# An adaLN transformer block on one core: the order of its first loads, of one gate row and of the last output tile

## The chip, the cores and the metric

The kernel runs on one core of a Trainium2 chip. The metric is the device time of one execution in microseconds (us). A core has five engines with queues of their own: PE (TensorE, matrix products into PSUM), DVE (VectorE), ACT (ScalarE), POOL (GpSimd) and SP (SyncE, which here only issues DMAs). ACT also issues some DMAs. All DMAs run on the same 16 DMA engines, in one queue for those that SP issues and another for those that ACT issues.

## The reference

One sequence of S = 2048 rows with D = 448 columns, bf16. The cut reference:

```python
mod = (silu(c) @ w_mod).reshape(1, 6, 1, -1)          # sa, ca, ga, sb, cb, gb: shifts, scales, gates
h = layernorm(x) * (1 + ca) + sa
# A: linear attention, 16 heads of 28; phi(p) = [softmax(p w_phi), softmax(-p w_phi)]
kv, z = phi_k^T v, sum(phi_k)                          # key-value sums, per head
o = (phi_q kv) / (phi_q z);  x = x + ga * (o @ wo)
h = layernorm(x) * (1 + cb) + sb
# B: gated MLP, F = 1792, halves of 896
z1, z2 = split(gelu(h @ w_in));  z2 = layernorm(z2)
g = w_sp @ z2 + b_sp                                   # mixes the 2048 rows
out = x + gb * ((z1 * g) @ w_out)
```

## The kernel before

The rows are cut into 16 tiles of 128. The body, `fast_path`, is a set of small functions ("steps"), each of which issues a few instructions, and a string, `ORDER`, in which every word is one call: `name:arguments@slot/engine`. The instructions of an engine run in the order of the words; nothing reorders them. A slot is a place in PSUM: A0, A1, A2 hold two banks each, B0 and B1 one; a step that writes a slot waits until the last reader of what was there is done. The engine letters are V (DVE), S (ACT), G (POOL), Y (SP). `ld:x/Y` is a load issued by SP, `ld:x/S` one issued by ACT. A DMA's issue also waits until the DMA eight places before it has landed, since there are eight semaphores for them.

The stages and the steps that matter here:

- **Start** (up to some 12 us). `du:n` are n warm-up matmuls of 256 columns on the zeroed tile `zero`; they compute nothing that is used. `ct` turns the row c by PE, `ce:1` to `ce:4` make silu(c) of it, `csA` and `ccA` are 16 one-column products each that give shift and scale as columns. `FTk`, `ETk`, `FSk`, `FCk`, `PFk`, `EPk` fold w_phi, shift and scale into the key weights `f_Wk`. `l1s`, `l1e`, `l1r`, `l1a` are the first layernorm (DVE statistics, POOL power, then the scaled tile into `f_xpad`), `X:i` turns tile i by PE into `f_hT`.
- **Key-value sums** (some 12 to 53 us). For every tile `kM` (keys), `kE`, `kF` (two exponentials on ACT), `kS` (sums on DVE), `kR`, `kP` (normalised keys, on DVE or POOL), `vM`, `vC` (values), `kA` (adds to the sums in PSUM). In between stand `qM:n`, the query products for half of the heads over 512 rows, with `qF:n` and `qE:n`, their exponentials on ACT. `gr:0` and `gr:1` are the two gate rows (four products of 448 columns each, from `f_wmg`), `ge` their copies to SBUF; `wos:k` multiplies gate row 0 into part k of wo, `wts:k` gate row 1 into part k of w_out. `T1` are DMA transposes of layernormed tiles.
- **Joint.** When `kA:15` is done, `KV` and `KZ` take the sums out of PSUM, and the attention starts.
- **Attention and z** (some 55 to 138 us). `nM:i` (numerators), `nX`, `nC`, `nS`, `nT`, `nA` (their weights, on ACT, DVE, POOL), `T2` (DMA transposes of the result), `wM:i` (times wo), `wR`, `wQ`, then the second layernorm (`l2R`, `l2r`, `l2a`, `T3`) and the products with w_in: `zM`, `yM`. `csB`, `ccB` are shift and scale for it. `W:t,u` are DMA transposes of blocks of w_sp from HBM.
- **Mixing and output** (from some 138 us). The products w_sp z2 with a seven-product scheme on 2x2 blocks (`P`, `d`, `x`), and `oM:t`, `oE:t`, `oD:t`: product of tile t with w_out (seven matmuls of 448 columns), the sum with x on DVE, the store.

Of the kernel before, what the change touches and what calls it, by code (L numbers as in the profile page):

```python
# [15 lines left out]
P = 128  # L16
# [469 lines left out]
SCv:1/G EPq:1/S XE:2/S l1s:6 PFq:0@B0 SCv:2/G X:3@A0 l1s:5 kM:2@B1 SCv:0/S XE:3/S l1s:7 ld:x4/Y l1s:9 EPq:0/S SCv:3/G l1e:4,8/G l1s:11 kS:0 vM:2@A1 vM:3@B0
EPq:2/S vC:2 ld:wmgb/Y kE:2 PFq:3@A0 EPq:3/S ld:wmga/Y l1s:8 kM:3@A2 kF:2 qM:1@A1 kR:1 ld:x5/S l1r:4,8 vM:0@B1 kR:0 kS:2 kE:3 kF:3 vM:1@A2 l1s:10 qE:1
l1a:4/G gr:1@A0 vC:0 l1s:13 l1a:5/G vC:1 ge:1 gr:0@B1 l1a:7/G kS:3 l1a:6/G vC:3 T1:4,6 kP:0/G T1:6,8 qF:1 kR:2 ge:0 qM:0@A2 qE:0 kP:1/G l1s:12 kM:5@B0
kM:4@B1 kF:4 kP:2/V vM:5@A1 kA:0@A0 kE:4 l1e:8,12/G l1r:8,12 kA:1@A0 kA:2@A0 ld:wo/Y vM:6@B1 l1a:8/G kF:5 kE:5 kR:3 kP:3/V l1s:14 l1s:15 kM:7@B0 l1a:9/G
qF:0 kS:5 vC:6 kM:6@A2 l1a:10/G kS:4 vC:5 l1a:11/G qM:2@A1 kF:6 kR:5 kF:7 kR:4 kE:6 kP:5/V ld:wcb/Y qF:2 T1:8,10 kP:4/V kS:6 kR:6 vM:7@B1 kE:7 T1:10,12  # L490
kA:3@A0 wos:0/G l1e:12,16/G vM:4@A2 l1r:12,16 vC:7 qE:2 l1a:15/G kM:9@B0 kF:9 l1a:12/V l1a:14/G kM:8@B1 l1a:13/V vM:9@A1 kE:9 kS:7 kR:7 kF:8 vC:4 kS:9
kE:8 kS:8 T1:12,14 kM:10@B0 kP:6/G kE:10 kP:7/G kR:8 kF:10 kA:4@A0 kA:5@A0 kM:11@B1 kE:11 T1:14,16 kS:10 vM:10@B0 kF:11 kS:11 kA:6@A0 vC:9 kA:7@A0 kM:12@B1
kP:8/G kR:10 kE:12 kR:9 kP:9/V kR:11 vC:10 kP:10/V kF:12 kS:12 kM:13@A1 kR:12 vM:8@A2 kM:15@B0 vC:8 kF:13 kP:11/G kM:14@B1 ld:wsb/Y kE:13 kS:13 kR:13 kE:14
W:0,6 kF:14 kE:15 kA:8@A0 kA:9@A0 kP:12/V kS:14 vM:11@A1 kF:15 kS:15 kA:10@A0 vM:14@B1 kR:14 vC:11 vM:15@B0 vC:14 vM:12@A2 vM:13@B1 vC:12 kA:11@A0 vC:13
kP:13/G kA:12@A0 kR:15 kP:14/V kP:15/V wos:2/V kA:13@A0 kA:14@A0 vC:15 kA:15@A0 KV:0/V KV:1/V KZ:0 ld:win0/S qM:3@A2 KZ:1 nM:0@A1 qE:3 ld:wout/S nM:1@A0
nX:0 nX:1 qF:3 nC:0 csB@B0 W:0,1 ld:win1/Y nC:1 nS:0 ccB@B1 nT:0 qM:4@A2 qE:4 nA:0/V nT:1 ecB nA:1/V wos:3/V qM:5@A1 nM:2@A0 qF:4 esB nX:2 nM:3@A2 nX:3
FB@B1 wos:1/V nC:2 qE:5 T2:0,1 nC:3 nS:1 FBc/S qF:5 nT:2 nA:2/G wM:0/S@B0 nT:3 SHw:3@B1 wR:0/S SCw:0,3/S T2:1,2 nM:5@A1 nX:5 nM:4@A0 nC:5 nX:4 nC:4 nA:3/V
wQ:0/S wM:1/S@B0 wR:1/S SHw:2@B1 SCw:2,1/S qM:6@A2 SCw:0,0/S SCw:3,1/G nS:2 nT:5 nT:4 T2:2,4 nM:6@A1 wQ:1/V qE:6 nX:6 nM:7@A0 nA:5/G nA:4/V nX:7 SCw:0,2/S
qF:6 nC:6 nC:7 nS:3 nT:7 wM:2/S@B0 wR:2/S wM:3/S@B1 wR:3/S qM:7@A2 wQ:2/S nT:6 wQ:3/S nA:6/V SCw:1,1/V SCw:1,0/V nM:9@A0 T2:4,6 qE:7 nM:8@A1 wM:5/S@B1
nX:8 nX:9 wM:4/V@B0 l2R:0,2/G l2r:0,2 l2a:0/G T3:0,1 l2a:1/V qF:7 nC:8 wR:5/S zM:0@A2 gt nA:7/G l2R:2,4/G nC:9 nS:4 nT:9 nT:8 zG:0 l2r:2,4 l2a:3/G T2:6,8  # L500
wR:4/V l2a:2/G nM:10@A0 T3:1,2 T3:2,4 wQ:5/S nX:10 nA:8/V SCw:3,0/G wM:6/V@B1 wR:6/V nM:11@A1 wQ:4/S nX:11 nA:9/V SCw:2,0/V l2R:4,6/G zM:1@A2 nC:11 nC:10
# [20 lines left out]
oM:4,0,7@B0 d:1,1,7 d:1,0,6 x:1,0,6/G oD:2/Y d:1,2,1 P:1,2,6 oD:3/Y d:1,2,2 P:1,2,2 oM:6,0,7@B1 P:1,2,7 x:1,0,8/V d:1,2,3 oE:6 P:1,1,3 d:1,1,6 P:1,2,5
oE:4 oD:4/Y oD:6/Y x:1,1,7/G P:1,1,4 x:1,1,6/G oM:7,0,7@B0 d:1,1,4 x:1,1,4/G d:1,2,4 x:1,2,4/G hint d:1,2,5 P:1,2,3 d:1,2,7 d:1,2,6 oE:7 x:1,2,6/G P:1,2,4
d:1,2,8,256,512 oD:7/Y oM:9,0,7@B0 oE:9 oD:9/Y d:1,2,8,0,256 oM:8,0,7@B1 oE:8 x:1,2,7/G oD:8/Y oM:10,0,7@B0 d:1,1,8 oE:10 x:1,1,8/G oD:10/Y oM:11,0,7@B1
oE:11 oD:11/Y x:1,2,8,0,256/G oM:12,0,7@B0 oE:12 oD:12/Y oM:13,0,7@B1 oE:13 oD:13/Y x:1,2,8,256,512/G oM:14,0,7@B0 oM:15,0,7@B1 oE:14 oD:14/Y oE:15 oD:15/Y
# [741 lines left out]
```

## Time and profile before

| | us |
|---|---|
| three timed runs | 249.0, 250.34, 250.72; median 250.34 |
| profiled execution, whole | 249.4 |
| its span, first to last instruction | 247.6 |
| PE busy | 240.5 (97%) |
| DVE, POOL, ACT busy | 182.5, 116.3, 104.8 |

The profile comes from one execution. Its times count from the start of the span. The rows of a timeline are: start, duration (both us), engine, line, operation, output and inputs, how many, and in brackets how long the engine sat idle before and what ended that. In the chain of work that ended last, each piece is what held up the next one.

### The profile page before, as it was taken

The numbers are of one execution on the slowest core, as the hardware profiler recorded it, in microseconds if no ns is written. First come the engines' busy times: TensorE is split into PE (matmuls) and PEld (weight loads), VectorE is DVE, ScalarE is ACT, GpSimd is POOL, SyncE is SP. The second block draws the span as 40 slices with busy tenths as digits, with TensorE's granted clock in tenths as the row PEclk, the third lists the DMA queues.
The fourth block names the chain that finished last, engine by engine and source line by source line (L and its number), as shares of the span: only waits on it lengthen the run. The fifth ranks groups of instructions, "written<-read, shape, count | busy, mean of one in ns | idle before, by whom it ended". The sixth has DMA issues, their size and how long they took to land.

```text
span 247.6 us, 4188 instructions
## 1 busy us (share of the span) xinstructions
PE 240.5 (97%) x1533; PEld 126.8 (51%) x1533; DVE 182.5 (74%) x369; ACT 104.8 (42%) x217; POOL 116.3 (47%) x175
## 2 busy tenths in 40 slices
PE   8999999999999999999999999999999999999992
PEld 5865556675665564444444444444444444444451
DVE  4689998967999989686571997798976363645562
ACT  2488887836999896866897100000000000000000
POOL 3667997500387668987509000521129610124430
PEclk9999999999999999999999999999999999999998
DMA  7973849746235787989990999000001000101022
GB/s 178 293 217 102 193 86 177 194 113 178 51 72 110 127 162 136 163 158 176 179 177 0 162 181 173 0 1 0 3 0 37 0 0 3 56 0 37 21 95 65
DMA packets 68207, 25.22 MB, mean 102 GB/s; under 512 B 58129, under 2 KB 67602, under 8 KB 68178
## 3 DMA queue, kind: packets, MB, share of 16 engines
q1 hardware_dynamic: 66210, 22.57, 46.1%
q10 hardware_dynamic: 1968, 2.29, 3.3%
q8 instruction: 14, 0.23, 0.4%
q14 instruction: 15, 0.12, 0.2%
HBM read 8.87 MB, written 1.84 MB: 43 GB/s over the span
## 4 chain that ended last, share of the span: by engine, by line
PE 85%; POOL 6%; ACT 3%; DVE 2%; DMA 1%; issue 1%; POOLq 0%
PE g_ps L1124 29%; PE o_ps L1159 9%; PE z_ps L1049 7%; PE q_ps L945 6%; PE k_ps L890 5%; PE v_ps L898 5%; PE g_ps L1145 5%; PE z_ps L1078 4%; PE x_ps L1005 4%; PE kvacc L921 3%; PE warm_ps L729 3%; PE num L973 2%; POOL f_zv L1035 1%; DMA f_hT<-f_xpad 1%; DVE f_z2n L1072 1%
## 5 line engine op out<-in xcount | busy, mean ns | idle before, releaser
L1133 DVE TENSOR_TENSOR f_zb<-g_ps,f_zb 128x512 f32<-128x512 f32 (+1 forms) x31 | 20.5, 670 | 17.1 <-PE g_ps L1124 16.7
L1124 PEld LDWEIGHTS <-f_z2n 128*128 128x128 bf16 x192 | 18.8, 98 | 22.7 <-issue 0.3
L1140 POOL TENSOR_TENSOR f_z1T<-f_zb,f_z1T 128x512 bf16<-128x512 f32 (+1 forms) x11 | 12.0, 1102 | 33.6 <-DVE f_zb L1133 33.6
L1049 PE MATMUL z_ps<-f_ar,f_hT 112*128 112x448 bf16 (+1 forms) x128 | 26.6, 352 | 0.0
L1140 POOL TENSOR_TENSOR f_z1T<-f_Sx,f_z1T 128x512 bf16<-128x512 f32 x6 | 8.0, 1332 | 39.3 <-DVE f_Sx L1133 39.3
L1078 PE MATMUL z_ps<-f_hT,f_ar 112*128 112x512 bf16 x112 | 26.1, 379 | 0.0
L1159 PE MATMUL o_ps<-f_wout,f_z1T 128*128 128x448 bf16 x112 | 22.5, 352 | 0.0
L1124 PE MATMUL g_ps<-f_ar 128*128 128x512 bf16 x96 | 22.4, 379 | 0.0
L1081 ACT ACTIVATE f_z1T<-z_ps,f_zb 128x512 bf16<-128x512 f32 x28 | 18.2, 684 | 5.2 <-PE z_ps L1078 5.1
L950 ACT ACTIVATE f_Eq<-q_ps 112x1024 bf16<-112x1024 f32 x16 | 16.3, 1032 | 5.8 <-PE q_ps L945 5.8
L1049 PEld LDWEIGHTS <-f_hT 112*128 112x128 bf16 (+1 forms) x128 | 12.2, 97 | 11.6
L1078 PEld LDWEIGHTS <-f_ar 112*128 112x128 bf16 x112 | 11.0, 98 | 12.6
L893 ACT ACTIVATE f_E<-k_ps 128x448 bf16<-128x448 f32 x32 | 15.8, 555 | 3.8 <-PE k_ps L890 3.7
L989 DVE TENSOR_TENSOR f_ar<-num,f_w 128x896 bf16<-128x896 f32 x16 | 17.0, 1087 | 0.4
L904 DVE TENSOR_REDUCE f_ksum<-f_E 128x32 f32<-128x896 bf16 x16 | 16.9, 1064 | 0.5 <-ACT f_E L893 0.4
L1124 PE MATMUL g_ps<-f_Eq,f_z2n 128*128 128x512 bf16 x72 | 16.5, 379 | 0.0
L1159 PEld LDWEIGHTS <-f_z1T 128*128 128x128 bf16 x112 | 11.0, 98 | 10.7
L1053 ACT ACTIVATE f_zb<-z_ps 128x896 bf16<-128x896 f32 x16 | 14.6, 913 | 4.1 <-PE z_ps L1049 3.8
L1162 DVE TENSOR_TENSOR f_xpad<-o_ps,f_x 128x448 bf16<-128x448 f32 x16 | 9.9, 622 | 8.0 <-PE o_ps L1159 7.9
L945 PE MATMUL q_ps<-f_hT,f_Wq 113*128 113x512 bf16 (+1 forms) x64 | 15.0, 379 | 0.6 <-ACT f_Eq L950 0.6
L1124 PEld LDWEIGHTS <-f_ar 128*128 128x128 bf16 x96 | 9.4, 98 | 11.1 <-DVE f_ar L1102 0.2
L1005 PE MATMUL x_ps<-f_ar 112*128 112x448 bf16 x64 | 14.1, 352 | 0.3 <-DVE f_x L1012 0.3
(202 smaller groups left out, 473.1 us busy)
## 6 DMA issues: line engine op xcount, KB each, us to landing
out_dram<-f_xpad SPq DMA_DIRECT2D x16, 112.0 KB, 1.7
f_wm<-in_w_mod_dram SPq DMA_DIRECT2D x4, 406.0 KB, 5.1
f_x<-in_A_x_dram SPq DMA_DIRECT2D x2, 448.0 KB, 7.8
f_wmg<-in_w_mod_dram SPq DMA_DIRECT2D x2, 392.0 KB, 9.9
f_ar<-in_B_w_in_dram SPq DMA_DIRECT2D x1, 784.0 KB, 5.6
f_ar<-in_B_w_in_dram ACTq DMA_DIRECT2D x1, 784.0 KB, 5.4
f_wout<-in_B_w_out_dram ACTq DMA_DIRECT2D x1, 784.0 KB, 5.6
f_bsp<-in_B_b_sp_dram SPq DMA_DIRECT2D x1, 512.0 KB, 5.7
```

What stands on the lines that cost most here:

```text
L904: nc.vector.tensor_reduce(out=ksum[:, i], in_=Er[i % NR][:].rearrange("p s (c f h) -> p (s c) h f", c=4, h=HP), axis=AX.X, op=ALU.add)
L945: nc.tensor.matmul(t[:, u, :], lhsT=Wq[0:KR[m], m, cc * CB:cc * CB + P], rhs=hT[0:KR[m], 4 * st:4 * st + 4, m, :], start=(m == 0), stop=(m ...
L950: nc.scalar.activation(out=Eq[st // 2][0:CB, 2 * c2:2 * c2 + 2, s, (st % 2) * 512:(st % 2 + 1) * 512], in_=ps["q" + str(n)][0:CB, :, :], f ...
L989: nc.vector.tensor_tensor(out=tr[i % 2][:], in0=numv(i)[:, :, :, 0:DH], in1=wr[i // 2 % 2][:, i % 2].unsqueeze(3).to_broadcast([P, 2, H, D ...
L1005: nc.tensor.matmul(t[:, 0, 0:D], lhsT=oT[0:CB, i % 4, cc, :], rhs=wo_s[0:CB, cc, :], start=(cc == 0 and not with_x), stop=(cc == KC - 1))
L1049: nc.tensor.matmul(t[:, hf, 0:D], lhsT=hT[0:KR[m], i, m, :], rhs=win_s[0:KR[m], m, FH + hf * D:FH + (hf + 1) * D], start=(m == 0), stop=(m ...
L1078: nc.tensor.matmul(t[:, 0, :], lhsT=win_s[0:CB, m, fc * P:(fc + 1) * P], rhs=hT[0:CB, 4 * st:4 * st + 4, m, :], start=(m == 0), stop=(m == ...
L1081: nc.scalar.activation(out=stage_b()["z1T"][:, fc, st * 512:(st + 1) * 512], in_=ps["y%d_%d" % (st, fc)][:, 0, :], func=ACT.Gelu_apprx_tan ...
L1124: nc.tensor.matmul(g, lhsT=sta[:, m, :], rhs=mov[:, m, :], start=(m == 0 and i in (1, 6, 7)), stop=(m == 7), skip_group_check=True)
L1133: nc.vector.tensor_tensor(out=o, in0=x, in1=y, op=ALU.add)
L1140: eng.tensor_tensor(out=z, in0=T[r][:, c0:c1], in1=z, op=ALU.mult)
L1159: nc.tensor.matmul(ps["o" + str(t)][:, 0, 0:D], lhsT=later["z1T"][:, FO[n], t * P:(t + 1) * P], rhs=wout_s[:, FO[n], :], start=(n == 0), s ...
```

## The change

`c` is loaded by ACT, ahead of the two first tiles of x, instead of by SP behind the key weights. The warm-up of 22 matmuls ahead of `ct` becomes eight ahead of it and nine behind it; the part of `zero` that the warm-up reads is cleared first of all on DVE. `csA` moves ahead of `X:0`. Gate row 1 (`gr:1`) and the load it needs (`ld:wmgb`) move from the first third of the key-value sums to the joint; `ccB` moves ahead of the first numerators. `qF:0`, `qE:0` and the other query exponentials come a few places earlier among the keys' work. `x5` is loaded by SP instead of ACT, `wmga`, `wmgb`, `wcb`, `wsb` by ACT instead of SP, `win1` by SP before the second pair of `T1`, `wout` by SP instead of ACT. The transposes `W:0,6` and `W:0,1` leave their early places for later ones, `W:1,3` and `W:1,7` come earlier. A few steps change engines (`l1a:13`, `nA:1`, `nA:10`, `l2a:5`, `SCw:2,0` from DVE to POOL; `nA:7` from POOL to DVE; `wQ:8` from ACT to DVE). The last output tile is computed, summed and stored in two parts of 256 and 192 columns.

The diff without the table, of which two words show the form:

```diff
-ORDER = """tbl du:8@B1 m2b/V ld:wk/Y du:3@A2 m2a/V du:11@A1 ld:c/Y ct@B0 ld:x1/S ...
+ORDER = """tbl ld:c/S du:8@B1 m2b/V ld:wk/Y ct@B0 m2a/V ld:x1/S ... m3 du:9@A1 FTk:1@B1 ...
-... oM:14,0,7@B0 oM:15,0,7@B1 oE:14 oD:14/Y oE:15 oD:15/Y
+... oM:14,0,7@B0 oP:15,0,256@B1 oE:14 oD:14/Y oP:15,256,448@B0 oF:15,0,256 oG:15,0,256/S oF:15,256,448 oG:15,256,448/Y
     def consts():
+        nc.vector.memset(zero[:, 0:256], 0.0)
         nc.gpsimd.memset(wk_raw[0:CB, :, D:D + 16], 0.0)
         ...
-        nc.vector.memset(zero[:], 0.0)
+    def oP(t, a, b, slot):
+        o = ps["op" + str(a)] = bank(slot, "o_ps")
+        for n in range(FC):
+            nc.tensor.matmul(o[:, 0, 0:b - a], lhsT=later["z1T"][:, FO[n], t * P:(t + 1) * P], rhs=wout_s[:, FO[n], a:b], start=(n == 0), stop=(n == FC - 1))
+    def oF(t, a, b):
+        nc.vector.tensor_tensor(out=later["ot"][t % 4][:, a:b], in0=ps["op" + str(a)][:, 0, 0:b - a], in1=x_sb[:, t, a:b], op=ALU.add)
+    def oG(t, a, b, eng):
+        eng.dma_start(out=outv[t][:, a:b], in_=later["ot"][t % 4][:, a:b])
```

Start, on ACT: the difference at the head of its queue (`f_c_row` is the row c; L657 and L656 load tiles 1 and 0 of x).

```order
 L732 ACT_TABLE_LOAD
 L732 ACTIVATE f_warm<-f_warm 128x1
+L655 DMA f_c_row<-in_c_dram 1x448
 L657 DMA f_x<-in_A_x_dram 128x448
 L656 DMA f_x<-in_A_x_dram 128x448
```

The load of c now stands ahead of the loads of x. On SP it leaves the place between the key weights and w_phi.

Joint, on ACT, before (L645 loads half of w_in, L675 w_out; L950 are query exponentials `qE`, `qF`; L977 are `nX`, the copies out of the numerators):

```order
L901 CAST f_vaug<-v_ps 128x16x28 x5
L645 DMA f_ar<-in_B_w_in_dram 112x2x1792
L950 ACTIVATE f_Eq<-q_ps 112x2x512
L675 DMA f_wout<-in_B_w_out_dram 128x7x448
L977 COPY f_Sx<-num 128x32 x2
L950 ACTIVATE f_Eq<-q_ps 112x2x512 x3
```

and now (L959 is `ge:1`, the copy of the gate row):

```order
L901 CAST f_vaug<-v_ps 128x16x28 x4
L950 ACTIVATE f_Eq<-q_ps 112x2x512
L977 COPY f_Sx<-num 128x32 x2
L950 ACTIVATE f_Eq<-q_ps 112x2x512
L959 CAST f_g_rep<-gr_ps 128x448
L950 ACTIVATE f_Eq<-q_ps 112x2x512 x2
```

The two loads have gone to earlier places, and the copy of gate row 1 stands behind the exponentials of `qM:3`. On PE, behind the eight products of `qM:3`, stood 16 of `nM`, 32 of `csB` and `ccB`, then `qM:4`; now stand 16 of `ccB`, 16 of `nM`, four of `gr:1`, 16 of `csB`, then `qM:4`.

Attention, on SP, now, behind the last `T1` (L872 with `f_ar` are `T2`, L1043 `T3`, L1086 `W`):

```order
L872 DMA_TRANSPOSE f_ar<-f_ar 128x4x128 x2
L872 DMA_TRANSPOSE f_ar<-f_ar 128x8x128
L1086 DMA_TRANSPOSE f_Eq<-in_B_w_sp_dram 128x8x128
L872 DMA_TRANSPOSE f_ar<-f_ar 128x8x128
L1043 DMA_TRANSPOSE f_hT<-f_xpad 128x4x128
```

Before, no L1086 stood here: `T2:4,6` followed `T2:2,4` directly, and seven transposes stood between `T2:2,4` and `W:1,3`.

More of the change, by code (lines that the diff above doesn't have):

```diff
@@ L486 @@
[L486 to L489, printed above, removed]
@@ L522 @@
[L522 to L525, printed above, removed]
+ORDER = """tbl ld:c/S du:8@B1 m2b/V ld:wk/Y ct@B0 m2a/V ld:x1/S l1s:1 ld:x0/S l1s:0 m1/G ld:phi/Y ce:1 m3 du:9@A1 FTk:1@B1 ce:2 l1e:1,2/G ld:wsa/Y du:2@A0 l1e:0,1/G
```

82 lines of the change are left out of this document (45 added, 37 removed).

## The prediction

> **What bounds the kernel now.** First the page: how busy each engine is, and the chain that ended last.
>
> ```profile
> span 247.6 us, 4188 instructions
> PE 240.5 (97%) x1533; PEld 126.8 (51%) x1533; DVE 182.5 (74%) x369; ACT 104.8 (42%) x217; POOL 116.3 (47%) x175
> PE 85%; POOL 6%; ACT 3%; DVE 2%; DMA 1%; issue 1%; POOLq 0%
> ```
>
> PE is busy for all but 7.1 of 247.6 us, and most of the chain is PE. So the change can win little: what PE stands idle, the warm-up work that PE does for nothing, and the stretch behind its last product. To see where the idle time lies I cut the span into stages:
>
> ```profile
> 12.00:53.00 41.00, 41.00 (x346) 25.05 (x345) 38.20 (x77) 33.52 (x65) 29.34 (x33) 1.00 0.67 150
> 53.00:58.00 5.00, 4.42 (x68) 3.03 (x66) 3.03 (x10) 2.11 (x4) 0.00 (x0) 1.00 0.86 233
> 58.00:103.00 45.00, 44.98 (x334) 25.40 (x333) 39.57 (x100) 38.18 (x92) 29.89 (x60) 1.00 0.63 118
> 103.00:138.00 35.00, 34.51 (x169) 16.13 (x168) 22.40 (x57) 26.90 (x50) 20.98 (x39) 1.00 0.79 142
> 138.00:243.00 105.00, 105.00 (x500) 48.72 (x498) 71.81 (x101) 0.00 (x0) 29.89 (x19) 1.00 0.23 43
> ```
>
> The columns are the stage, its length, then busy time and instructions of PE, its weight loads, DVE, ACT, POOL, the granted clock, the DMA share and GB/s. PE never rests in the key-value sums (12 to 53); it rests 0.58 us at the joint and 0.49 us from 103 to 138. In the sums DVE is busy 38.20 of 41 us as well, so PE is only just the slowest there. The start is read from the chain in order of time (start, duration):
>
> ```profile
> 1.23 4.88 PE warm_ps L729 x22
> 6.11 0.46 PE ct_ps L740 x4
> 6.57 0.62 PE tps L822 x8
> ...
> 8.04 0.66 PE warm_ps L729 x6
> ```
>
> The 22 warm-up matmuls take 4.88 / 22 = 0.222 us each, the six at 8.04 take 0.66 / 6 = 0.110 us each, for the same 256 columns: PE works at half speed until somewhere between 6 and 8 us, though the granted clock of the page does not show that.
>
> **The start: +0.1 us.** The change takes five warm-ups away (5 x 0.222 = 1.1 us) and starts the rest some 0.14 us sooner, since half of `zero` is cleared. But it puts a wait for c behind the first eight. When does c land, and what then sets the pace? The issues and those who wait:
>
> ```profile
> 0.92 0.38 ACTq L657 DMA_DIRECT2D f_x<-in_A_x_dram  x1
> 1.17 0.38 SPq L655 DMA_DIRECT2D f_c_row<-in_c_dram  x1
> 1.34 0.44 ACTq L656 DMA_DIRECT2D f_x<-in_A_x_dram  x1
> 4.78 0.63 DVE L856 BATCH_NORM_STATS2 f_st<-f_x 128x6 f32<-128x448 bf16 x1 [2.01 <-DMA f_x<-in_A_x_dram]
> 8.65 0.71 POOL L867 TENSOR_SCALAR f_xpad<-f_x,f_nm,f_rs 128x448 bf16<-128x448 bf16 x1
> 9.42 0.40 PE L880 MATMUL xt_ps<-f_ident,f_xpad 128*128 128x128 bf16 x4
> f_x<-in_A_x_dram ACTq DMA_DIRECT2D x2, 112.0 KB, 4.0
> out_dram<-f_xpad SPq DMA_DIRECT2D x16, 112.0 KB, 1.7
> ```
>
> c takes the issue slot of the first tile of x, at 0.92. Such an issue needs 4.0 us to land at the start and 1.7 in a quiet stage, so c lands between 2.6 and 4.9; I take 3.9, near the first row, since c is small but lies in the same stage. PE is through its eight warm-ups at 1.1 + 8 x 0.222 = 2.9, waits about 1 us, needs 0.46 for `ct` and 9 x 0.222 = 2.0 for the other nine, and comes to the key weights (`FTk:1`) at 6.4: against 6.57 now, nothing won. With 2.6 it would come at 5.4, with 4.9 at 7.4.
>
> Coming sooner would not help. POOL ends the first-layernorm tile at 8.65 + 0.71 = 9.36 and PE turns it (`X:1`) at 9.42: PE and POOL arrive there together. POOL's chain hangs on the two tiles of x, for which DVE waited until 4.78, and these now stand one issue (0.42 us) further back on ACT. If that issue is hidden, as when the transfers themselves set the landing, `X:1` stays where it is; if it shows, everything moves by 0.4. So the start runs from -0.1 to +0.8, and I take +0.1, near the first case, since a row of 0.9 KB adds nothing to the transfers. The move of `csA` ahead of `X:0` only fills PE's time. Of SP's loads, phi, shift and scale start one issue earlier, which nothing waits for.
>
> **The joint: -0.5 us.** In order of time:
>
> ```profile
> 23.49 1.51 PE gr_ps L956 x8
> ...
> 53.39 1.75 PE q_ps L945 x8
> ...
> 55.16 0.40 ACT f_Eq L950
> 55.56 0.52 issue
> 56.08 0.27 ACT f_Sx L977 x2
> 56.35 0.93 ACT f_Eq L950
> ...
> 57.32 3.63 PE q_ps L945 x16
> 60.95 0.87 PE num L973 x16
> 57.32 3.63 PE L945 MATMUL q_ps<-f_hT,f_Wq 113*128 113x512 bf16 x16 [0.58 <-ACT f_Eq L950]
> ```
>
> `qM:3` ends on PE at 55.14. `qM:4` needs the same slot, and ACT frees it only after two exponentials and the two copies between them, at 57.3: 2.2 us, in which PE has 16 products of `nM` (0.87) and the columns of `csB` and `ccB` (2 x 0.40, as the 16 at the start take 0.38 to 0.40), and then idles for 0.58. Now `gr:1` (half of 1.51 = 0.76) stands there too: 0.87 + 0.80 + 0.76 = 2.43 us, more than ACT's 2.2. The idle time is gone, `qM:4` comes 0.2 later after `qM:3`, and the sums are 0.76 shorter: 0.76 - 0.25 = 0.5 us won, no more than the idle time that there was. ACT's copy of the gate row (0.53 us at 24.28 for the other one) falls into the time in which it waits for `qM:4`.
>
> This holds if everything before `kA:15` follows by 0.76 us. DVE has 41 - 38.20 = 2.8 us of rest there, and it loses one layernorm tile (0.4) to POOL, so it can. The sooner query exponentials only trade places on ACT (33.5 of 41 us). Bounds: 0 where DVE or ACT hold the sums back, 0.58 at best. `wmgb`, issued by ACT near the end of the sums, some 8 us ahead of its use, has room by the 4 to 5.7 us that loads need in this profile; w_out's load leaves 55 us, where DMA is busiest, for earlier.
>
> **The tail: -0.25 us.** The last rows:
>
> ```profile
> 233.87 9.28 PE o_ps L1159 x49
> 243.17 0.62 DVE L1162 TENSOR_TENSOR f_xpad<-o_ps,f_x 128x448 bf16<-128x448 f32 x1 [0.70 <-PE o_ps L1159]
> 234.44 0.42 DVE L1133 TENSOR_TENSOR f_zb<-g_ps,f_zb 128x256 f32<-128x256 f32 x1
> ```
>
> PE's share stays: 448 columns cost 9.28 / 49 = 0.189, and 256 and 192 cost 0.110 and about 0.083, so seven of each are 1.35 instead of 1.32. Behind the last product the sum runs over 192 columns instead of 448. 448 take 0.62 and 256 take 0.42, so 192 take about 0.35: 0.27 won, 0.03 lost. The sum over 256 columns ends before the last product does (it starts 0.6 us ahead and takes 0.42), and its store is ACT's. The last store has 128 rows of 384 bytes instead of 896; no store of this size is in the trace, and it could land 0.1 sooner or, if short rows cost more, 0.3 later than the 1.7 of the row above. Range -0.4 to +0.1.
>
> **Attention and z: 0.** PE rests only 0.02 us there, so moved steps can only cost. The move that could is `W:1,3` ahead of `T2:4,6` on SP:
>
> ```profile
> 69.82 1.24 SPq L872 DMA_TRANSPOSE f_ar<-f_ar  x1
> 74.03 1.68 PE L1005 MATMUL x_ps<-f_ar 112*128 112x448 bf16 x8
> f_ar<-f_ar SPq DMA_TRANSPOSE x1, 3.0
> ```
>
> `T2:4,6` is issued at 69.82, lands 3.0 later at 72.8, and is used at 74.03: 1.2 us to spare. `W:1,3` needs `nM:7` done (about 69.4) and holds SP for some 1.3 us, so `T2:4,6` is issued near 70.7 and lands at 73.7 or, if W's own transfer is still running, later: 0 to 0.9 us of stall, of which I take 0, with little to spare. On POOL four tiles more and one less are work of 1 us each or less in a stage where POOL is busy 29.89 of 45. The 0.49 us from 103 to 138 stays, since its chain starts at PE and moves with it.
>
> **The sum.** +0.1 - 0.5 - 0.25 + 0 = -0.65 us. For the profiled execution that is 247.6 - 0.65 = 246.95 of span and 249.4 - 0.65 = 248.75 in all. The median of the timed runs, 250.34, lies 0.94 above the profiled execution; the mean of all four is 249.87, and from that the sum gives **249.2**, my forecast.
>
> **A rule that speaks against the start.** The rows say that PE's speed doubles after some 5 to 6 us of unbroken warm-up. The Trainium skill, "TensorE: Matmul & The Clock Gate", Part 1, says that the clock stays halved until the array has been busy through a window of about 3.4 us that runs freely, without regard to the kernel's start. The 0.222 and 0.110 us agree with it. By it, a wait of 1 us for c in the middle of the warm-up can spoil a window and put the doubling off by up to 3.4 us.
>
> **The rivals.** (1) *The doubling comes late.* As a mechanism of this kernel: whatever PE does between 6.4 and 12.3 at half speed costs its time again. Ahead of `X:1` these are eight warm-ups (8 x 0.111 = 0.9) and the turning of weights (0.62 + 0.57, perhaps a third more), behind it five warm-ups, the folds and the first key product (0.88): 1.3 us if speed comes at 9, 2.3 if at 12. Against it: only 1 us of wait, and nine warm-ups behind it. It decides where c lands later than 3.9 or so. With the other terms it gives -0.75 + 1.3 = +0.55, up to +1.5: 250.4 to 251.4, slower than before. Chance 0.2. (2) *DVE holds the sums*, its rest being spread over many short waits: the joint gives nothing, 249.7. Chance 0.15. (3) *`T2:4,6` is late* by 0.9: 250.1. Chance 0.1. (4) *The start gains*: c lands at 2.6 and x is not held up, so PE is ahead by 1.1 and POOL by a little, with the sums' and the tail's best: -1.5 to -2, 248.0. Against it stands POOL's 9.36. Chance 0.1. The forecast has 0.45.
>
> **Range and chances.** About 1%, 2.5 us, is what measurement of this kernel can tell from no change; the three runs differ by 1.7. The bounds of the terms add up to -0.1 - 0.58 - 0.4 = -1.1 and +0.8 + 0 + 0.1 + 0.9 = +1.8; with the spread of the runs, 247.6 to 251.1. Faster by over 1% needs less than 247.8, which only (4) with a low median gives: 0.13. Slower by over 1% needs 252.8, the far end of (1): 0.07. Within 1%: 0.80.
>
> **What would show it.** Start: PE's wait at `ct` (1 us expected), `FTk:1` near 6.4, `X:1` near 9.4 to 9.8, and 0.110 us per warm-up behind `FTk:1`; 0.22 there is rival 1. Joint: no idle ahead of `qM:4`, and `qM:3` some 0.7 earlier against the first key product; idle PE between 12 and 53 is rival 2. Attention: idle ahead of the `wM` at 74 is rival 3. Tail: 0.35 us for the last sum. I would be most wrong if a load now issued by ACT landed late, for PE waits in order: the gate row's at the joint, or `wmga` at some 23 us.

## The result, and the profile after

| | before | changed | ratio, 95% interval |
|---|---|---|---|
| timed runs | 249.57 us (20, 248.8 to 250.76) | 251.14 us (20, 250.42 to 251.86) | 1.0059 [1.0047, 1.0072] |
| traced execution | 249.4, span 247.6 | 251.28, span 249.4 | |

The forecast was 249.2 us, from 247.6 to 251.1. The kernel became 1.6 us slower. (Of all runs below, one execution of e4 and one of e8 took 511 and 647 us; the ratios leave them out.) The traced executions differ by 1.8 us of span, so one trace against the other can say where. Four places on PE and the end of the span, in time order, with the shift against before:

| | before | changed | shift |
|---|---|---|---|
| `X:1`, second tile turned | 9.42 | 11.14 | +1.72 |
| first key product `kM:1` | 12.10 | 13.82 | +1.72 |
| `qM:4` at the joint | 57.32 | 58.58 | +1.26 |
| end of PE's last product | 243.15 | 244.55 | +1.40 |
| end of the span | 247.6 | 249.4 | +1.8 |

So the start lost 1.72 us, the joint gave 0.46 back, and the last tile lost some 0.55: 0.15 on PE and 0.4 behind it. Attention, z and mixing kept their length.

**The start.** The timeline of the changed kernel (start, duration, engine, what; in brackets the idle time before and what ended it), much the same rows as the prediction showed of before:

```profile
1.08 0.54 ACTq L655 DMA_DIRECT2D f_c_row<-in_c_dram  x1
1.18 0.47 SPq L649 DMA_DIRECT2D f_phi<-in_A_w_phi_dram  x1
1.66 0.39 ACTq L657 DMA_DIRECT2D f_x<-in_A_x_dram  x1
1.70 1.02 SPq L652 DMA_DIRECT2D f_wm<-in_w_mod_dram  x2
2.08 0.44 ACTq L656 DMA_DIRECT2D f_x<-in_A_x_dram  x1
4.32 0.53 PE L740 MATMUL ct_ps<-f_one,f_c_row 1*112 1x1 bf16 x4 [1.40 <-DMA f_c_row<-in_c_dram]
5.36 0.63 DVE L856 BATCH_NORM_STATS2 f_st<-f_x 128x6 f32<-128x448 bf16 x1 [2.58 <-DMA f_x<-in_A_x_dram]
7.38 0.63 DVE L856 BATCH_NORM_STATS2 f_st<-f_x 128x6 f32<-128x448 bf16 x1 [1.17 <-DMA f_x<-in_A_x_dram]
8.81 1.20 PE L729 MATMUL warm_ps<-f_zero 128*128 128x256 bf16 x6
10.26 0.38 PE L880 MATMUL xt_ps<-f_ident,f_xpad 128*128 128x128 bf16 x4
10.37 0.72 POOL L867 TENSOR_SCALAR f_xpad<-f_x,f_nm,f_rs 128x448 bf16<-128x448 bf16 x1
11.14 0.40 PE L880 MATMUL xt_ps<-f_ident,f_xpad 128*128 128x128 bf16 x4
...
13.82 1.04 PE L890 MATMUL k_ps<-f_Wk,f_hT 113*128 113x448 bf16 x4
```

Two things are to be seen. The first tile of x lets DVE start at 5.36 (4.78 before), but the second, x0, only at 7.38: DVE waits 1.17 us for it, where before it went from the one tile to the other. POOL's scaled tile and PE's `X:1` follow at 10.37 and 11.14. And the six warm-ups at 8.81 take 0.20 us each: PE is still at half speed when they begin, where before it was at full speed by 8 us. The chain that ended last takes the first of the two:

```profile
2.08 5.28 DMA f_x<-in_A_x_dram
7.36 0.02 issue
7.38 0.64 DVE f_st L856
```

x0 was issued 0.74 us later than before (2.08 against 1.34) and needed 5.28 us to land, where it needed 4.1 before.

**The joint, and the sums before it:**

```profile
57.21 0.92 PE L956 MATMUL gr_ps<-f_wmg,f_scb 112*128 112x448 bf16 x4
57.97 0.54 PE L764 MATMUL cf_ps<-f_scol,f_wm 112*128 112x1 bf16 x16
58.58 1.68 PE L945 MATMUL q_ps<-f_hT,f_Wq 113*128 113x512 bf16 x7
...
12.00:53.00 41.00, 40.76 (x358) 24.93 (x355) 38.06 (x77) 34.53 (x67) 30.18 (x35) 1.00 0.75 178
```

The gate row stands between the numerators and `csB`, and the bracket with 0.58 us of idle time ahead of `qM:4` is gone. The stage from 12 to 53 us has PE busy 40.76 of 41; the 0.24 us lie ahead of `kM:1`, in the start that now lasts longer.

**The last tile,** and the transfers of 244.5 to 246.5 us (queue q8 carries instructions, not data; its row has packets, MB and the share of the 16 engines):

```profile
242.92 1.62 PE L1170 MATMUL o_ps<-f_wout,f_z1T 128*128 128x256 bf16 x14
243.12 0.62 DVE L1162 TENSOR_TENSOR f_xpad<-o_ps,f_x 128x448 bf16<-128x448 f32 x1 [0.70 <-PE o_ps L1159]
243.88 0.42 DVE L1173 TENSOR_TENSOR f_xpad<-o_ps,f_x 128x256 bf16<-128x256 f32 x1
244.34 0.38 ACTq L1176 DMA_DIRECT2D out_dram<-f_xpad  x1
244.57 0.36 DVE L1173 TENSOR_TENSOR f_xpad<-o_ps,f_x 128x192 bf16<-128x192 f32 x1 [0.26 <-PE o_ps L1170]
244.96 0.33 SPq L1176 DMA_DIRECT2D out_dram<-f_xpad  x1
...
243.08 1.47 PE o_ps L1170 x14
...
q8 instruction: 1, 0.02, 4.7%
out_dram<-f_xpad ACTq DMA_DIRECT2D x1, 64.0 KB, 3.5
out_dram<-f_xpad SPq DMA_DIRECT2D x1, 48.0 KB, 3.0
```

The last sum takes 0.36 us instead of 0.62, and the store follows at once. But the two stores need 3.5 and 3.0 us to land. The same view of before, 243.1 to 245.1 us, has no q8 row, and its last store needs 2.2; q8's row lies a stage earlier, at 242.2 to 244.2:

```profile
out_dram<-f_xpad SPq DMA_DIRECT2D x1, 112.0 KB, 2.2
...
q8 instruction: 1, 0.02, 5.2%
```

### The profile page after: what moved, and what is told of

The parts are those of the page before. It is cut to its first block, busy times and chain, and to the rows that moved or that the text cites. A ratio compares the mean times of both kernels' runs of the same rounds, so it can differ in the third digit from the quotient of the medians.

```text
span 249.4 us, 4194 instructions
## 1 busy us (share of the span) xinstructions
PE 241.0 (97%) x1535; PEld 127.3 (51%) x1535; DVE 181.4 (73%) x368; ACT 104.9 (42%) x215; POOL 119.4 (48%) x179
## 4 chain that ended last, share of the span: by engine, by line
PE 79%; POOL 6%; ACT 4%; DMA 4%; DVE 3%; issue 1%; ACTq 0%; POOLq 0%
PE g_ps L1124 29%; PE o_ps L1159 8%; PE q_ps L945 6%; PE z_ps L1049 5%; PE k_ps L890 5%; PE z_ps L1078 5%; PE v_ps L898 5%; PE g_ps L1145 5%; PE x_ps L1005 3%; PE kvacc L921 3%; DMA f_x<-in_A_x_dram 2%; PE num L973 2%; DMA f_hT<-f_xpad 2%; ACT f_ar L1017 1%; ACT f_zb L1053 1%; POOL f_xpad L1038 1%
## 5 line engine op out<-in xcount | busy, mean ns | idle before, releaser
L1159 PE MATMUL o_ps<-f_wout,f_z1T 128*128 128x448 bf16 x105 | 21.2, 352 | 0.0
L950 ACT ACTIVATE f_Eq<-q_ps 112x1024 bf16<-112x1024 f32 x16 | 16.2, 1030 | 5.5 <-PE q_ps L945 5.5
L1159 PEld LDWEIGHTS <-f_z1T 128*128 128x128 bf16 x105 | 10.3, 98 | 10.0
L1162 DVE TENSOR_TENSOR f_xpad<-o_ps,f_x 128x448 bf16<-128x448 f32 x15 | 9.2, 622 | 7.3 <-PE o_ps L1159 7.2
L890 PE MATMUL k_ps<-f_Wk,f_hT 113*128 113x448 bf16 (+1 forms) x64 | 14.4, 352 | 0.0
```

The lines of the kernel that those rows point to most:

```text
L890: nc.tensor.matmul(t[:, 0, 0:D], lhsT=hT[0:KR[m], i, m, :], rhs=Wk[0:KR[m], m, :], start=(m == 0), stop=(m == KC - 1))
L1159: nc.tensor.matmul(ps["o" + str(t)][:, 0, 0:D], lhsT=later["z1T"][:, FO[n], t * P:(t + 1) * P], rhs=wout_s[:, FO[n], :], start=(n == 0), s ...
```

## Experiments on the start

Every run was timed against the kernel before, on the same chip.

| run | c | PE's warm-up | x0 | `X:1` | time | ratio to before |
|---|---|---|---|---|---|---|
| changed | first on ACT | 8, wait, 9 | third on ACT | 11.14 | 251.14 | 1.0059 [1.0047, 1.0072] |
| e1 | second on SP | 22 | second on ACT | 9.63 | 250.39 | 1.0035 [1.0013, 1.0057] |
| e2 | third on ACT | 8, wait, 9 | second on ACT | 12.77 | 253.0 | 1.0132 [1.0097, 1.0167] |
| e3 | first on ACT | 22 | third on ACT | 11.32 | 253.93 | 1.0154 [1.0114, 1.0194] |
| e8 | first on SP | 8, 9 | second on ACT | 9.89 | 249.92 | 1.0009 [0.9987, 1.003] |
| e9 | first on ACT | 22, then 22 more | third on ACT | 11.75 | 252.05 | 1.0081 [1.0053, 1.011] |
| e13 | first on ACT | 8, wait, 9 | second on SP | 10.10 | 250.41 | 1.0038 [1.0014, 1.0063] |

**e1: the start of before, the rest as changed.**

```diff
-tbl ld:c/S du:8@B1 m2b/V ld:wk/Y ct@B0 m2a/V ld:x1/S l1s:1 ld:x0/S ... m3 du:9@A1 FTk:1@B1 ...
+tbl du:8@B1 m2b/V ld:wk/Y du:3@A2 m2a/V du:11@A1 ld:c/Y ct@B0 ld:x1/S l1s:1 ld:x0/S ... m3 FTk:1@B1 ...
```

The place of `csA` and the clearing of `zero` are those of before as well.

> The changed kernel with the start of before: c back on SP's queue behind the key weights, the 22 warm-ups ahead of ct unbroken, zero cleared whole. In the trace of the changed kernel X:1 came 1.72 us later than before and the joint gave 0.48 back, so if the start carries the loss, X:1 is back at 9.4 us and the time falls by 1.7 us, to about 249.4 (0.999 of before). Rival: the loss lies in the spread of transfers later on; then less than 0.8 us comes back (250.3 or more).

`X:1` was back at 9.63 and the span at 247.5 (median of the runs 247.7), 1.7 us below the changed kernel's: the start carries the loss. The time fell by less, to 250.39, because the time outside the span was 2.3 to 2.9 us in this kernel's runs where it is 1.8 in those of before and changed. That remains unexplained (see the end); the span is what the start decides.

**e2 and e3: each half of the start undone alone.** In e2 ACT issues `x1`, `x0`, `c` in this order; in e3 all 22 warm-ups stand ahead of `ct`:

```diff
 e2
-tbl ld:c/S du:8@B1 m2b/V ld:wk/Y ct@B0 m2a/V ld:x1/S l1s:1 ld:x0/S l1s:0
+tbl ld:x1/S ld:x0/S ld:c/S du:8@B1 m2b/V ld:wk/Y ct@B0 m2a/V l1s:1 l1s:0
 e3
-tbl ld:c/S du:8@B1 m2b/V ld:wk/Y ct@B0 m2a/V ... m3 du:9@A1 FTk:1@B1
+tbl ld:c/S du:8@B1 m2b/V ld:wk/Y du:3@A2 m2a/V du:11@A1 ct@B0 ... m3 FTk:1@B1
```

> The changed kernel with one thing altered: ACT issues the two tiles of x first and c third; PE still waits for c after eight warm-ups. Queue theory (x0 lands late because it is issued third): x0 is issued near 1.4 and lands near 5.4 as before, X:1 is at 9.4 to 9.8, the time 249.4 to 249.8 although PE's speed doubles as late as in the changed kernel or later. Clock theory (the wait for c puts the doubling from 6.7 to about 9.8 us, and that holds X:1 up): c lands at 5 or later, the doubling comes at 10 or later, and X:1 stays at 11 us or worse, 251.1 or more.

> The changed kernel with the opposite half undone: c stays first on ACT's queue, but PE runs all 22 warm-ups without a break ahead of ct, as before. Clock theory: the doubling is back at 6.5 to 6.9 us and X:1 at 9.4 to 9.8, the time 249.4 to 249.8. Queue theory: the doubling is early, but x0 still lands near 7.3 us and X:1 stays at 11.1, the time 251.0 to 251.2.

Both are slower than the changed kernel: e2 goes the way of the clock theory, e3 that of the queue theory and beyond. The timeline of e2:

```profile
5.89 0.59 DVE L856 BATCH_NORM_STATS2 f_st<-f_x 128x6 f32<-128x448 bf16 x1
6.54 0.53 PE L740 MATMUL ct_ps<-f_one,f_c_row 1*112 1x1 bf16 x4 [3.61 <-DMA f_c_row<-in_c_dram]
11.03 1.06 PE L729 MATMUL warm_ps<-f_zero 128*128 128x256 bf16 x6
12.77 0.39 PE L880 MATMUL xt_ps<-f_ident,f_xpad 128*128 128x128 bf16 x4
```

x0 is early, as the queue theory said: DVE begins on it at 5.89 without a wait. But c, 0.9 KB behind two tiles, is late: PE waits 3.61 us for it, still works at half speed at 11 us (1.06 / 6 = 0.18 us a warm-up), and `X:1` comes at 12.77 through PE's own order. Here the wait for c and the late speed bind, and the tile has long been ready. Now e3, timeline and stages (the third column from the end is the granted clock):

```profile
7.57 0.63 DVE L856 BATCH_NORM_STATS2 f_st<-f_x 128x6 f32<-128x448 bf16 x1 [1.20 <-DMA f_x<-in_A_x_dram]
9.00 0.54 PE L764 MATMUL cf_ps<-f_scol,f_wm 112*128 112x1 bf16 x16 [1.50 <-DVE f_scol L753]
10.41 0.40 PE L880 MATMUL xt_ps<-f_ident,f_xpad 128*128 128x128 bf16 x4 [0.87 <-DVE f_xpad L867]
11.32 0.61 PE L880 MATMUL xt_ps<-f_ident,f_xpad 128*128 128x128 bf16 x4
14.86 1.70 PE L890 MATMUL k_ps<-f_Wk,f_hT 113*128 113x448 bf16 x4
...
11.00:16.00 5.00, 5.00 (x61) 3.96 (x61) 2.99 (x11) 2.41 (x5) 1.47 (x7) 0.51 1.09 314
16.00:18.00 2.00, 2.00 (x19) 1.80 (x18) 0.77 (x3) 0.98 (x2) 1.73 (x3) 0.53 0.04 7
```

PE was early and at full speed, and x0 still landed late: DVE waits 1.20 us for it until 7.57 and `X:1` stays at 11.32, as the queue theory said. What came on top nobody had expected: PE, done early, rested for 1.5 us ahead of 9.0 and 0.9 ahead of 10.4, and then the granted clock fell to a half from 11 to 17.9 us. The first key products take 0.37 us per 448 columns instead of 0.19. So the wait for c in the changed kernel probably did one good thing: it kept PE's work together until x came. One of e3's six executions kept a granted clock of 0.998. It has no trace, but its span was 249.3 us, the changed kernel's 249.4: without the wait for c and without the later loss of speed, the late x0 seems to cost as much as the whole changed start.

**e13: x0 early, c and PE as changed.** SP issues x0 right behind the key weights, ahead of phi, shift and scale.

```diff
-tbl ld:c/S du:8@B1 m2b/V ld:wk/Y ct@B0 m2a/V ld:x1/S l1s:1 ld:x0/S l1s:0
+tbl ld:c/S du:8@B1 m2b/V ld:wk/Y ld:x0/Y ct@B0 m2a/V ld:x1/S l1s:1 l1s:0
```

> The changed kernel with the tile x0 issued by SP, right behind the key weights and ahead of phi, shift and scale (at 1.2 us; 2.1 on ACT in the changed kernel); c stays first on ACT and PE waits for it after eight warm-ups. If x0 landed at 7.4 because it stood behind phi, shift and scale in the transfers, it lands at 5.3 to 5.8 here, and X:0 and X:1 wait only for PE and its late clock: X:1 at 9.7 to 10.7, depending on where the doubling falls between 7.7 and 11 us; the time is 250.0 to 250.7. If the landing follows the load on all transfers whatever the order, X:1 stays at 11.1 and the time at 251.1.

```profile
6.32 0.59 DVE L856 BATCH_NORM_STATS2 f_st<-f_x 128x6 f32<-128x448 bf16 x1
10.10 0.39 PE L880 MATMUL xt_ps<-f_ident,f_xpad 128*128 128x128 bf16 x4
...
1.08 3.06 DMA f_c_row<-in_c_dram
```

DVE goes from x1 to x0 without a wait, and `X:1` comes at 10.10, 1.0 us sooner than in the changed kernel. The time, 250.41, is 0.7 below it, inside the expectation. Here x0 changed its queue and its time of issue (1.18) along with its place. But the other traces agree: in all nine in which the load of the shift (406 KB) is issued ahead of x0, x0 needs 5.0 to 5.5 us to land, in all nine in which x0 goes ahead of it 3.8 to 4.6, on ACT's queue too (e2: 4.2). And x1, behind c on ACT's queue, needs 3.9 us here as it needed 3.8 before. So it was x0's place behind the shift's load that made it late, not c's place ahead of x1. The chain that ended last now goes through the landing of c (last row) and PE's warm-ups: the 0.7 us that are left against before are the wait for c and the late speed.

**e8: both early.** c goes first on SP's queue, ahead of the key weights (`ld:c/Y` as the first load; x1 and x0 first on ACT).

> The changed kernel with c issued first on SP's queue, ahead of the key weights, and the two tiles of x first on ACT's as before; PE still waits for c after eight warm-ups, and the rest is as changed. So x is early (it should land at 5.1 to 5.7 us, its layernorm ready at 8.8 and 9.5) while PE's speed still doubles late, at 8 to 11 us. If the late clock alone held X:0 and X:1 up, X:1 comes at 10.6 to 11.1 and the time is 250.7 to 251.1; if it was x's late landing alone, X:1 comes at 9.6 and the time is 249.4 to 249.6. X:1 between 10.0 and 10.6 would say that each of the two costs about 1 us by itself, the other being hidden behind it.

```profile
2.86 0.53 PE L740 MATMUL ct_ps<-f_one,f_c_row 1*112 1x1 bf16 x4
6.13 0.63 DVE L856 BATCH_NORM_STATS2 f_st<-f_x 128x6 f32<-128x448 bf16 x1 [0.64 <-DMA f_x<-in_A_x_dram]
9.89 0.40 PE L880 MATMUL xt_ps<-f_ident,f_xpad 128*128 128x128 bf16 x4
```

This was to show the late clock alone, and missed: c had landed before PE was through its eight warm-ups, so nothing waited. It shows another thing: with c and x both early the start costs 0.5 us over before's, and the whole kernel is level with before. Here c, issued at 0.72, was there within 2.1 us; issued third on ACT (e2) it took 4.5.

**e9: x late, PE kept busy.** e3 with `du:6` made `du:28`.

> The opposite: c first on ACT's queue (x0 lands near 7.3 us as in the changed kernel), the 22 warm-ups unbroken, and 22 more warm-ups ahead of csA, so that PE neither waits for c nor rests while it waits for x0. If PE's rest made the kernel with c first and no wait 2.7 us slower than the changed one (speed halved again from 11 to 18 us), that loss is gone here: no 0.373 us per 448 columns in the first key products, X:1 at 11.1 to 11.3, span 249.2 to 249.6. If the loss there had another cause, the span stays above 251. And as the clock is early here, a span no lower than the changed kernel's 249.4 says that x0's landing alone is worth the 1.7 us of the start.

The key products take their normal 0.19 us again, so it was PE's rest that halved its speed in e3. The rest of the expectation failed. The warm-ups ran to 11 us and held `X:0` up themselves, which shifted `X:1` to 11.75; and in the traced execution (252.8 us, 0.75 above the median) a wait appeared that neither kernel has:

```profile
83.86 1.02 PE L1078 MATMUL z_ps<-f_hT,f_ar 112*128 112x512 bf16 x4 [0.83 <-DMA f_hT<-f_xpad]
```

**Which of the two held the changed kernel?** The speed doubles at another moment in every execution (the 22 unbroken warm-ups of before's start take 3.98 to 4.88 us in six traces), and that makes an experiment of its own: in the trace of e5 (below; its start is the changed one) it came sooner.

```profile
8.76 0.82 PE L729 MATMUL warm_ps<-f_zero 128*128 128x256 bf16 x6
11.12 0.40 PE L880 MATMUL xt_ps<-f_ident,f_xpad 128*128 128x128 bf16 x4
```

Here the six warm-ups run at full speed from 8.76 us on (0.82 us, as in the timeline of before), in the changed kernel they took 1.20, and `X:1` is at 11.12 and 11.14. So x0's landing sets the pace in these two. The late speed lies right behind it, as e2 and e13 show: without x0 it would still cost 0.7 us. But the two are nearly level. Seven traces have the changed start (changed, e4, e5, e11, e14, e15, e16), all with `X:1` at 10.97 to 11.24; the chain that ended last goes through x0's landing in five of them, but in e4 and e14, where the six warm-ups take 1.13 and 1.48 us, through the landing of c and PE's warm-ups.

## Experiments on the joint

**e7: start and tail of before, the rest as changed.** As e1, and the last tile in one part.

> The start of before and the last output tile in one part; the joint, the attention order and the moved loads stay as changed. If the tail of the changed kernel costs 0.5 us (PE's end to the span's end took 4.85 us there against 4.45 before, and PE's last tile 0.15 more), this is 0.5 us faster than the kernel with the start alone undone, and 0.5 us faster than before through the joint: about 249.0, 0.998 of before. Rival: the late landing of the last stores is chance, and the two runs agree within 0.2 us.

248.88 us (12 runs, 248.46 to 250.02), 0.9967 [0.9947, 0.9988] of before: the joint and what moved with it are worth 0.3%, 0.5 us by the traces (span 247.1 against 247.6). It is the best kernel of this study.

**e10: the gate row behind `qM:5`,** on e7:

```diff
-nM:0@A0 nC:1 gr:1@B0 nX:0 ... csB@B1 qM:4@A2 qM:5@A0 ge:1 qF:4 qE:4
+nM:0@A0 nC:1 nX:0 ... csB@B1 qM:4@A2 qM:5@A0 gr:1@B0 qF:4 ge:1 qE:4
```

> The kernel with start and tail undone (248.88 us, 0.9967 of before), and of the joint one thing altered: PE computes the gate row gr:1 behind qM:5 instead of ahead of qM:4, and ACT copies it one place later. If the joint's gain is that gr:1 fills PE's wait for ACT's exponential (0.72 us idle before, 0.20 left now), the wait is back at 0.9 to 1.0 us ahead of qM:4, gr:1 takes its 0.76 elsewhere, and the time is 0.75 higher, about 249.6. Rival: the gain came from somewhere else (fewer or shorter waits in attention, the moved loads); then the time stays within 0.2 of 248.9.

```profile
58.23 3.63 PE L944 MATMUL q_ps<-f_hT,f_Wq 113*128 113x512 bf16 x16 [0.82 <-ACT f_Eq L949]
62.65 0.53 ACT L958 CAST f_g_rep<-gr_ps 128x448 bf16<-128x448 f32 x1 [1.47 <-PE gr_ps L955]
64.16 0.58 PE L972 MATMUL num<-f_ar,f_Eq 112*128 112x120 bf16 x8 [1.13 <-ACT f_Eq L949]
...
64.00:70.00 6.00, 5.84 (x64) 3.83 (x64) 3.75 (x10) 4.03 (x12) 1.03 (x1) 0.72 0.02 4
```

The wait ahead of `qM:4` is back with 0.82 us, so the gate row did fill it. The time, 251.1 (1.0065 [1.0046, 1.0084] of before), rose by 2.2 instead of 0.75, because the copy `ge:1` now stands ahead of the second exponential on ACT and waits 1.47 us for PE's gate row: PE then waits another 1.13 us for that exponential. From `qM:3` to the `fb_ps` products behind the joint PE needs 10.7 us, in e7 8.7. The traced execution itself took 253.66 us, the other four 250.67 to 251.41 at clocks of 0.996 to 0.998: in it PE's clock also fell to a half twice (11.0 to 14.4 us, and after that rest; 0.72 on average from 64 to 70 us), which the median does not contain. The expectation had named the copy's new place, but not that the exponential behind it would wait.

**e12: PE's rest ahead of `X:0` filled,** e7 with `du:6` made `du:12`.

> The kernel with start and tail undone, with six more warm-ups (0.66 us) in PE's rest of 0.81 us ahead of X:0. In 2 of its 12 runs the granted clock was 0.990 instead of 0.996 to 1.000 and the time 1.0 us higher. If that is PE's rest at 8 us costing it its speed for a while, no run here shows it, and the median is the same, 248.8 to 248.9. Rival: the rest has nothing to do with it, and one run in five or six still shows 0.990.

249.67 us, 1.0013 [0.9991, 1.0035]. No run of the ten had a granted clock under 0.996, which fits, though none of 10 against 2 of 12 is too few to tell, and the kernel was 0.8 us slower than e7. Its trace has the wait of e9 again: PE waits 0.7 us at 81.6 for a transpose that took long,

```profile
76.73 4.72 DMA f_hT<-f_xpad
```

and in e9 and e12 a 16 KB transfer of instructions lies just there (at 80.0 and 79.3 us), where in e7 and the changed kernel it comes at 82.7 and 83.8, after the transpose. Before has one at 80.2, with another order of transposes and no such wait. That more warm-ups move that transfer, and it holds up the transpose, fits this but was not tried by itself.

## Experiments on the last tile

| run | products | sum | stores | time | ratio to before | PE's end to span's end |
|---|---|---|---|---|---|---|
| e4, e14 | one part | one | one | 250.27, 250.46 | 1.0018, 1.0022 | 4.3, 4.4 |
| e11, e16 | one part | two | two | 250.93, 250.83 | 1.0058, 1.0052 | 4.5, 4.6 |
| e5 | two parts | two | one | 251.07 | 1.005 | 5.0 |
| changed, e15 | two parts | two | two | 251.14, 251.03 | 1.0059, 1.0061 | 4.9, 4.8 |

All have the start and joint of the changed kernel; the intervals reach 0.0012 to 0.0024 to either side. e4 and e5 ran together, and e14, e15 and e16.

```diff
 e4, e14
-oP:15,0,256@B1 oE:14 oD:14/Y oP:15,256,448@B0 oF:15,0,256 oG:15,0,256/S oF:15,256,448 oG:15,256,448/Y
+oM:15,0,7@B1 oE:14 oD:14/Y oE:15 oD:15/Y
 e5
-... oF:15,0,256 oG:15,0,256/S oF:15,256,448 oG:15,256,448/Y
+... oF:15,0,256 oF:15,256,448 oD:15/Y
 e11, e16 (oF reads the slot of oM)
+oM:15,0,7@B1 oE:14 oD:14/Y oF:15,0,256 oG:15,0,256/S oF:15,256,448 oG:15,256,448/Y
```

> The changed kernel with the last output tile in one part, start and joint as changed. By the trace of the changed kernel the split costs 0.15 us on PE (0.11 of it a wait for DVE to empty the slot of the second part), wins 0.26 in the last sum, and its stores end the span 0.2 to 0.4 later behind PE's last product: 0.2 to 0.5 us faster than the changed kernel, about 250.8. Rival: the late stores were chance, and the split wins its 0.1: 251.25.

> The changed kernel with the last tile's products and sums in two parts, but one store of the whole tile on SP's queue. If two short stores cost more than one (384 and 512 bytes a row, two queues), this is 0.3 to 0.5 us faster than the changed kernel and 0.1 faster than the kernel with the tail undone, about 250.75. If the cost lies in the split products, it is as slow as the changed kernel, 251.1.

> The changed kernel with the last tile's products in one part, as before, but its sum and its store still in two. In the traces with split products a 16 KB fetch of instructions starts 0.3 us behind PE's last product and makes the last pieces of the stores late; with whole products it starts 0.9 us ahead of it. If the split products move that fetch, it is back at 0.9 ahead here, PE's end to the span's end is 4.3 to 4.6 us, and the time is 250.3 to 250.5, as with the tail undone or 0.16 above (the last sum ends that much later: 0.42 + 0.36 against 0.62). If the split sums and stores move it, it stays behind PE's end and the time is 250.9 to 251.1.

The tail costs more than nothing: whole, it is faster. The single store (e5) wins nothing, so with split products the two short stores are not the reason. e11 came out as slow as the changed kernel, while its trace was only 0.2 us longer behind PE than e4's; and e4's traced execution was 0.5 us longer than its other runs. So the three were set side by side again:

> The changed kernel with the last tile whole, a second time. If the tail is worth 0.9 us, this is again near 1.002 of before and its trace ends X:1 at 11.0 to 11.2 us as in the changed kernel, the whole difference lying behind 240 us. If a shorter start made the difference, either X:1 comes sooner than 11 us here, or the time is now 250.6 to 250.8, 0.5 below the changed kernel as the first traces say.

> The changed kernel again, beside the others: 1.0059 of before, about 251.1; PE's end to the span's end 4.6 to 5.0 us, X:1 at 11.1.

> Products whole, sum and stores of the last tile in two, a second time. If the tail's cost lies in the split sums and stores, it is again as slow as the changed kernel within 0.2 us. If the trace is right (PE's end to the span's end 0.2 longer than with the whole tile), it lies 0.2 above the kernel with the tail undone, and 0.3 to 0.5 below the changed one.

Timed together: 250.46 whole, 250.83 with sums and stores split, 251.03 with everything split. So the tail costs 0.57 us by these medians, as the traces add up to (0.15 on PE, 0.4 behind it). How it divides is not settled: by the medians some 0.35 come with the second sum and store (between the two forecasts of e16) and 0.2 with the split products, by the traces 0.16 and 0.35. The ratios to before, with their wide intervals, would give 1.0 us for the whole, in this round as in the first.

**e17: sums and stores split on e7.**

> The kernel with start and tail undone (0.9967 of before), with only the sum and the stores of the last tile in two. If these cost 0.7 us by themselves, it is at 249.6, level with before; by the traces it is 0.16 to 0.2 above, 249.05 to 249.1, as the last sum ends 0.16 later and the stores land as before.

249.16 us, 0.9982 [0.9965, 0.9998]: 0.3 above e7, nearer to the traces' 0.2 than to 0.7, though the two were not timed together.

What makes the split products slower behind PE is seen in the q8 row. With split products (changed, e5) the transfer of instructions starts some 0.3 us behind PE's last product and is on the DMA engines while the last stores are; with whole products it starts 0.8 to 0.9 us ahead of PE's end (0.1 in e17), and is over before the stores' data move. In e16, whole products and split stores, the view of 243.4 to 245.4 us has it:

```profile
q8 instruction: 1, 0.02, 5.2%
...
out_dram<-f_xpad ACTq DMA_DIRECT2D x1, 64.0 KB, 2.2
out_dram<-f_xpad SPq DMA_DIRECT2D x1, 48.0 KB, 2.2
```

The same two short stores land after 2.2 us there, and after 3.5 and 3.0 in the changed kernel. The other traces agree: SP's last store lands after 2.5 to 3.1 us in the nine with split products and after 1.8 to 2.4 in the nine with whole ones. That the late transfer holds the stores is inferred from this, and no run moved the transfer by itself; why it starts later with split products is open.

## Why the prediction was wrong

**The start: +0.1 was forecast, at most +0.8; it was +1.72.** This is the step that failed. Two sentences of it: that x stands "one issue (0.42 us) further back on ACT", so that everything moves by 0.4 if that shows; and that "of SP's loads, phi, shift and scale start one issue earlier, which nothing waits for". c left SP's queue, so SP's loads of phi, shift and scale went out 0.3 to 0.4 us sooner, while x0 went out 0.74 us later. (Not 0.42: c's issue moved x0 by 0.58, and ACT's first issue came at 1.08 instead of 0.92, 0.04 us behind DVE's clearing of `f_warm`, ahead of which the clearing of `zero` now stands.) Together they changed places: before, x0 was issued (1.34) ahead of phi (1.60) and shift and scale (1.98); now it is issued (2.08) behind phi (1.18) and the first of those two (1.70), 430 KB together. The bound of 0.8 counted ACT's queue alone. x0 landed 1.9 us later, and `X:1` 1.7. e13 and the landing times of the other traces show that this place, not c, was the cause: x0 back ahead of them took 1.0 us off `X:1`.

The smaller steps of the start were near: c was expected at 3.9 and PE's wait at 1 us; it was 4.3 and 1.40, and `FTk:1` came at 6.68 instead of 6.4.

**Rival 1, the doubling comes late** (250.4 to 251.4, 0.2), holds the measured time, but is not its cause in the traced execution. The mechanism was there: 0.20 us a warm-up at 8.81. But with the doubling early (e5) `X:1` came no sooner. It is the second of two conditions, nearly level with the first (in e4 and e14 it is the one that binds), so removing one leaves the other; e2 is what it does by itself when c is later still, and e13 prices it at 0.7 us, below the 1.3 to 2.3 that rival 1 gave.

**The joint: right.** -0.5 forecast, -0.46 measured, with no idle ahead of `qM:4` but 0.2 us; e10 brings the wait back. Rival 2 did not come: from the first key product to `qM:3` the sums take 40.4 us instead of 41.1: 0.71 sooner, close to the 0.76 of the sum, so DVE let them through. The load for the gate row was in time, though the "4 to 5.7 us that loads need" left out longer rows of the same page, 7.8 us for x and 9.9 for the gate rows.

**The tail: wrong in sign,** -0.25 forecast with +0.1 as its end, +0.55 measured. The durations were right: 0.36 us for the sum of 192 columns (0.35 forecast), 0.082 for a product of that width (0.083). Two terms were missing. `oP:15,256,448` takes slot B0, which holds tile 14 until DVE's sum of it ends at 243.74, so PE stands for 0.11 us between the parts: before, the one part of tile 15 had slot B1 to itself. And the last stores: up to 0.3 us later was the bound, from their size; they came 1.3 and 0.8 us later than 2.2, and e5 shows that size was not the reason.

**Attention and z: right,** 0. `T2:4,6` is in time (no idle at the `wM` near 75 us), rival 3 did not come. Other short waits changed places: one of 0.27 us in front of a `z_ps` product at 96.19 is new, one of 0.26 at 103.72 is gone.

The sum, with what was measured: 1.72 - 0.46 + 0 + 0.55 = +1.8, the difference of the spans. The upper end of the range does not follow from its own terms: their bounds add up to +1.8, and 249.87 + 1.8 is 251.7, not 251.1. That +1.8 also came is luck: the start went 0.9 and the tail 0.45 over their bounds, the joint and the attention stayed 0.5 and 0.9 under theirs.

## What to carry to other kernels

When a load leaves one queue for another, write down the issue times of all loads on both queues, before and after: a load that another one passes can land later by more than its issue moved (here 1.9 us for 0.74), and a load that nobody waits for can still stand in front of one that somebody does. A wait taken into the start of the program is judged by whichever comes last, the data or PE's speed; undoing one alone can make it worse, so undo them one by one and both. Splitting the last step for a shorter tail pays only if slots, stores and the transfers still on the way leave the shorter end free.

## What the hardware showed that was not expected

- **PE's speed is lost again after a short rest.** In e3 PE rested 1.5 and 0.9 us between 7.3 and 10.4 us and ran at half clock from 11 to 17.9 (0.51 on average from 11 to 16, 0.53 from 16 to 18); in e10 it rested 1.13 us ahead of 64.16 and the clock averaged 0.72 from 64 to 70 us. The Trainium skill, "TensorE: Matmul & The Clock Gate", Part 1, has windows of 3.4 us that run freely and a clock that falls after an idle one. The length agrees: 6.8 us in e3 are two such, and (1 - 0.72) x 6 / 0.5 = 3.4 us in e10 are one. That the window must be idle does not: in e10 PE was busy for 2.3 of the 3.4 us from 62.2 to 65.6, and at 65.6 the clock fell. In e7, with a rest of 0.7 us near 8 us, 2 of 12 runs had a clock of 0.990 and 1.0 us more; in e12, with that rest filled, none of 10. The kernel before shows it as well: 4 of the 19 runs timed beside e14 to e17 had clocks of 0.989 to 0.993 and took 0.8 to 1.2 us more than its median.
- **A row of 0.9 KB can be slow.** c took 2.1 us at most when issued first of all on SP (e8), 3.1 to 3.5 first on ACT (e13, e5), 4.5 behind two tiles of x on ACT (e2).
- **Transfers of instructions** of 16 KB share the DMA engines with the data, at places that differ from kernel to kernel: in e7 and e17, with the same products, the last but one starts 0.9 and 0.1 us ahead of PE's end. Two waits (e9, e12) and the late last stores coincide with such a transfer.
- **Time outside the span** was 1.8 us in most kernels, 2.3 to 2.9 in e1 and e3 and 2.0 in e12. These three have 1539 or 1540 matmuls, the others 1535 or fewer, but e9 with 1562 has 1.8. It is not explained.
